# Attention with two MLPs on one core: loads and first conversions of K and V tied to the low part of P

## The chip, the cores and the metric

The kernel runs on one core of a Trainium2 chip. The metric is the device time of one execution in microseconds (us). The core has a matrix engine (TensorE, PE in the profile; its weight loads are PEld), a vector engine (VectorE, DVE), a scalar engine (ScalarE, ACT), GpSimd (POOL), a sync engine (SyncE, SP) that here issues nearly all transfers, and 16 DMA engines that carry them out.

## The reference

Four batches of 8 heads, 576 positions, head size 64. Causal attention is mixed with a memory read-out, and the result (2304 rows of 512) goes through two MLPs of width 2048.

```python
scores = scale * np.matmul(q, k.transpose(0, 1, 3, 2))
...
local = np.matmul(a, v)
...
return (g * mem_out + (1 - g) * local).astype(np.float32)
...
h = x @ w_in
g = np.maximum(h, 0.0) + np.log1p(np.exp(-np.abs(h)))
return (g @ w_out).astype(np.float32)
...
r = np.maximum(h, 0.0)
g = r * r
return (g @ w_out).astype(np.float32)
```

`a` is the softmax of the masked scores, and the MLP weights come as 64-bit floats.

## The kernel before

Every operand is split into a high 16-bit part and a low part (the rest), and a product is made of three matmuls (high by high, high by low, low by high).

The 2304 rows are 18 chunks of 128, numbered from 0: two batches at a time, four full chunks of each in turn, then one chunk of the two remainders (chunks 8 and 17). A chunk attends to its own and the earlier chunks of its batch, so chunks 0 to 8 and 9 to 17 are two halves that share nothing. A chunk is worked on in attention steps: 2 steps for chunks 0, 1, 9 and 10, 4 for 2, 3, 11 and 12, 8 for the others, 104 in all.

A step (`attn_step`) records `emit_s` (scores on PE, L311; mask and row maximum on DVE, L316; exponential on ACT, L320), then the part of the preparation of the next chunk that falls into it, then `emit_p`: the high part of P on ACT (L334), the low part on DVE (L335), and the transpose of both by DMA (L197, tile PT). Four steps later `emit_pv` multiplies by V (L359), and after every fourth head `emit_x` finishes rows of x (xt, xf, xn, L385 to L397).

The preparation of a chunk (`prep_part`) has four parts, at the quarters of the chunk before: K (`prep_k`: high part on ACT, L230, low part on DVE, L231, transpose into KT by DMA), q, phi of q, and V (`prep_v`: ACT L238, DVE L239). After a part has used its raw tile (rawk, rawq, rawv, one buffer of each; a second one for the first K) it asks for the next chunk's load (`load`, L181, on SP). KT and V have 9 buffers each.

The first MLP's weights come in 32 pieces of 512 KB (tile wst, three buffers). A piece is decoded in three DVE instructions (wcv, L428 to L430), its high part W is made on ACT (L432), its low part on DVE (L433). The first MLP's matmuls (L445 to L447 into hps, L462 to L464 into xps, L507 to L509 into xacc) are recorded in units between the attention steps, by a table of costs. For chunks 0 and 1 transposes are made on PE (L203) and copied by ACT (L204), x of these chunks among them; later ones go by DMA. When attention has ended its memory is given to the weights of the second MLP, which are loaded and decoded in the same way; the second MLP follows.

The program is recorded in this order and then ordered anew: a scheduler keeps a list of ready instructions per engine and takes them by priority (`tc.high_priority`), with a model of their times. The order it makes is fixed; on the chip each engine executes its own list in order, and semaphores hold it where its data is not there. `tc.add_manual_dep` with `NoSync` gives the scheduler an edge between two instructions and makes no semaphore. The kernel before has such an edge in `emit_pv`, to the entry of `p_lo` two steps after its own.

Of the kernel before, what the change touches and what calls it, by code (L numbers as in the profile page):

```python
# [13 lines left out]
AF = mybir.ActivationFunctionType  # L14
# [19 lines left out]
TP = 2  # L34

KVB = 9
SPB = 2
WCB = 2
NST = 3
# [11 lines left out]
def kernel(  # L51
# [15 lines left out]
    pe, act, dve, pool, sp = nc.tensor, nc.scalar, nc.vector, nc.gpsimd, nc.sync  # L67
# [58 lines left out]
    for m in (mask[:, 0, 3 * P:], mask[:, 1, EMAX // 2 - P:EMAX // 2]):  # L126
        pool.affine_select(
            out=m, in_=m, pattern=[[-1, P]], compare_op=ALU.is_ge, fill=-8.0e9, base=0, channel_multiplier=1,
# [35 lines left out]
    raw, qT, phiT, KT, V, Mt, Pt, PT, pvt, cs_t = ({} for _ in range(10))  # L164

    def segs(g):
        x = CH[g]
        if len(x) == 2:
            return [(x[0], P * x[1], 0, P)]
        return [(2 * x[0] + i, 4 * P, i * R, R) for i in range(2)]  # L170

    def lo_eng(g):
        return dve if g < LOE else pool

    def load(nm, g, pool_=None):
        if g >= NC or (nm, g) in raw:
            return
        src = {"q": q, "k": k, "v": v}[nm]
        t = (pool_ or att).tile([P, H, D], F32, name="raw" + nm, bufs=1)
        for b, s0, r0, n in segs(g):  # L180
            sp.dma_start(out=t[r0:r0 + n], in_=src[b, :, s0:s0 + n, :].rearrange("h p d -> p h d"))  # L181
        raw[nm, g] = t
    def load_m(g):
        for b, s0, r0, n in (segs(g) if g < NC else []):
# [6 lines left out]
    def transp(g, out, in_, lim):  # L191
        nblk = in_.shape[1] // P
        if g >= lim:
            step = nblk if nblk <= 12 else nblk // 2
            for a in range(0, nblk, step):
                e = a + step
                sp.dma_start_transpose(out=out[:, a:e], in_=in_[:, a * P:e * P])  # L197
            return
        for a in range(0, nblk, 8):
            e = min(nblk, a + 8)  # L200
            ps = mm.tile([P, 8, P], F16, tag="mm", name="tps")
            for i in range(a, e):
                pe.transpose(ps[:, i - a], in_[:, i * P:(i + 1) * P], ident)  # L203
            act.activation(out[:, a:e], ps[:, :e - a], AF.Copy)  # L204
# [22 lines left out]
    def prep_k(g):  # L227
        r = raw.pop(("k", g))
        kn = att.tile([P, H, 2, D], F16, name="kn")
        act.activation(kn[:, :, 0, :], r, AF.Copy)  # L230
        lo_eng(g).tensor_tensor(kn[:, :, 1, :], r, kn[:, :, 0, :], ALU.subtract)  # L231
        KT[g] = att.tile([P, H, P], F16, name="KT", bufs=KVB)
        transp(g, KT[g], kn.rearrange("p h t d -> p (h t d)"), TP)

    def prep_v(g):
        r = raw.pop(("v", g))
        V[g] = att.tile([P, 2, H, D], F16, name="V", bufs=KVB)
        act.activation(V[g][:, 0], r, AF.Copy)  # L238
        dve.tensor_tensor(V[g][:, 1], r, V[g][:, 0], ALU.subtract)  # L239

    def prep_m(g):
# [44 lines left out]
    def emit_s(g, h0):  # L286
# [34 lines left out]
                pf, pf, AF.Exp, bias=cs[:, 0, h:h + 1], scale=-1.0, accum_out=cs[:, 1, h:h + 1],  # L321
            )
        Pt[g, h0] = p

    p_lo = []

    def emit_p(g, h0):
        G, ext = GRP[g], EXT[g]
# [108 lines left out]
    def unit_h(kb, fp):  # L437
        ps = mm.tile([P, 2, NB], F32, tag="mm", name="hps")
        x = x_at(kb)
        for i in range(2):  # L440
            f = 2 * fp + i
            o = ps[:, i]
            for c in range(NCC):
# [3 lines left out]
                pe.matmul(o, wl, x[:, c], start=False, stop=(c == NCC - 1))  # L447
        a = w1p.tile([P, 2, NB], F32, name="spa", bufs=SPB)
        act.activation(a, ps, AF.Abs)
# [68 lines left out]


    load("k", 0)  # L520
    load("q", 0)
    load("k", 1, stage)
    load("v", 0)
    gates()
# [7 lines left out]
    def prep_part(g, part):  # L532
        if g >= NC:
            return
        if part == 0:
            prep_k(g)
            load("k", g + 1)
        elif part == 1:
            prep_q(g)
        elif part == 2:  # L540
            prep_phi(g)
            load("q", g + 1)
        elif part == 3:
            prep_v(g)
            load("v", g + 1)
            prep_m(g)
            load_m(g + 1)

    prep_k(0)
    prep_q(0)  # L550
    prep_phi(0)
    load("q", 1)
    prep_v(0)
    load_m(0)
    load("v", 1)
# [460 lines left out]
```

## Time and profile before

| what | value |
|---|---|
| timed runs | 957.05, 959.77, 960.59 us (median 959.77) |
| span of the profiled execution, first to last instruction | 953.8 us |
| mean granted clock of TensorE | 0.970 |
| PE busy | 869.4 us (91%) |
| PE weight loads busy | 728.7 us (76%) |
| DVE busy | 737.9 us (77%) |
| ACT busy | 612.4 us (64%) |
| queue that SP issues to, share of the 16 DMA engines | 52.1% |

The page gives the profiled execution as its span; the timed runs include what lies around it. Busy shares are means over stages with different limits: the attention and the first MLP run together up to about 540 us, the second MLP's weights are decoded up to about 640 us, and the second MLP fills the rest.

### The profile page before, as it was taken

What the parts mean: (1) busy time and instruction counts of PE and PEld (TensorE: products, weight loads), DVE (VectorE), ACT (ScalarE), POOL (GpSimd) and SP (SyncE); (2) the same over time, 40 slices, a digit from 0 to 9 for tenths busy, and PEclk for the clock granted to TensorE, in tenths of its full rate; (3) what the DMA queues carried; (4) which work ended last, traced back from release to release, by engine and by line L of the source; (5) the groups of instructions that cost most, each with busy time, mean ns of one, the idle gap of its engine ahead of it and who ended that gap; (6) DMA issues with size and microseconds to landing.
All of it is one profiled execution on the core that took longest, in us unless ns stands there. A gap on an engine that the chain in (4) does not pass through costs nothing.

```text
span 953.8 us, 24659 instructions
## 1 busy us (share of the span) xinstructions
PE 869.4 (91%) x10380; PEld 728.7 (76%) x10380; DVE 737.9 (77%) x1490; ACT 612.4 (64%) x1144; POOL 2.2 (0%) x10
## 2 busy tenths in 40 slices
PE   4434999989999889999999998999999999999998
PEld 3233889878878788899988887544695999999993
DVE  7997999878647767575855599999998998867640
ACT  7864888778759677786957466563356656544530
POOL 0000000000000000000000000000000000000000
PEclk9955999999999999999999999999999999999999
DMA  9999997778698986547664575610000000000001
GB/s 235 234 239 221 219 190 150 118 131 134 101 150 162 182 134 109 96 82 116 92 103 79 133 215 162 200 41 23 23 2 12 13 23 2 24 24 2 24 13 34
DMA packets 285024, 101.25 MB, mean 106 GB/s; under 512 B 248048, under 2 KB 284400, under 8 KB 284912
## 3 DMA queue, kind: packets, MB, share of 16 engines
q1 hardware_dynamic: 284672, 99.65, 52.1%
q8 instruction: 81, 1.33, 0.6%
q14 instruction: 31, 0.25, 0.1%
q10 hardware_dynamic: 240, 0.02, 0.0%
HBM read 48.78 MB, written 4.72 MB: 56 GB/s over the span
## 4 chain that ended last, share of the span: by engine, by line
PE 47%; DVE 9%; ACT 6%; DMA 5%; issue 3%; SPq 1%; DVEq 0%; ACTq 0%
PE h2ps L821 4%; PE h2ps L822 4%; PE h2ps L823 4%; PE ops L883 3%; PE ops L882 3%; PE ops L881 3%; PE hps L447 2%; PE hps L446 2%; PE hps L445 2%; PE s_ps L311 2%; PE xps L463 2%; PE xps L464 2%; PE xps L462 2%; PE h2ps L738 1%; PE ops L918 1%
## 5 line engine op out<-in xcount | busy, mean ns | idle before, releaser
L445 PE MATMUL hps<-x,W 128*128 128x256 f16 x576 | 157.1, 275 | 5.8 <-ACT x L204 4.4
L446 PE MATMUL hps<-x,W 128*128 128x256 f16 x576 | 157.8, 275 | 0.5 <-ACT x L488 0.3
L447 PE MATMUL hps<-x,W 128*128 128x256 f16 x576 | 157.8, 275 | 0.0
L463 PE MATMUL xps<-g,W 128*128 128x256 f16 x512 | 138.7, 273 | 2.1 <-DVE g L456 2.1
L462 PE MATMUL xps<-g,W 128*128 128x256 f16 x512 | 137.1, 273 | 3.4 <-ACT g L455 3.4
L464 PE MATMUL xps<-g,W 128*128 128x256 f16 x512 | 138.7, 273 | 0.0
L311 PE MATMUL s_ps<-KT,qT 128*128 128x128 f16 (+2 forms) x992 | 80.1, 224 | 38.6 <-DVE cs L316 38.1
L320 ACT ACTIVATE Pt<-Pt,cs 128x128 f32<-128x128 f32 (+4 forms) x144 | 84.0, 584 | 43.0 <-DVE cs L316 42.8
L311 PEld LDWEIGHTS <-qT 128*128 128x128 f16 (+1 forms) x992 | 58.4, 105 | 50.2 <-issue 43.9
L335 DVE TENSOR_TENSOR p<-Pt,p 128x512 f16<-128x512 f32 (+2 forms) x104 | 69.2, 665 | 33.7 <-ACT p L334 33.6
L316 DVE CUSTOM_DVE_ANT_0 Pt<-s_ps,mask 128x128 f32<-128x128 f32 (+3 forms) x128 | 61.7, 482 | 9.1 <-PE s_ps L311 8.6
L334 ACT ACTIVATE p<-Pt 128x512 f16<-128x512 f32 (+2 forms) x104 | 62.9, 605 | 5.7 <-DMA PT<-p 4.5
L446 PEld LDWEIGHTS <-W 128*128 128x128 f16 x576 | 56.7, 98 | 12.7 <-issue 6.1
L432 ACT ACTIVATE W<-wcv 128x512 f16<-128x512 f32 x64 | 40.0, 625 | 40.3 <-DVE wcv L430 31.0
L447 PEld LDWEIGHTS <-W 128*128 128x128 bf16 x576 | 56.7, 98 | 7.3 <-issue 0.8
L445 PEld LDWEIGHTS <-W 128*128 128x128 f16 x576 | 56.7, 99 | 6.5
L359 PE MATMUL pvt<-V,PT 128*128 128x64 f16 (+1 forms) x1392 | 59.4, 197 | 0.5 <-DMA PT<-p 0.5
L456 DVE TENSOR_TENSOR g<-spa,g 128x512 f16<-128x512 f32 x72 | 49.2, 685 | 12.9 <-ACT g L455 12.7
L452 DVE SCALAR_TENSOR_TENSOR spa<-hps,spa 128x512 f32<-128x512 f32 x72 | 49.3, 686 | 11.6 <-ACT spa L451 11.5
L462 PEld LDWEIGHTS <-W 128*128 128x128 f16 x512 | 49.9, 98 | 9.4 <-issue 4.2
L464 PEld LDWEIGHTS <-W 128*128 128x128 bf16 x512 | 50.1, 98 | 8.1 <-issue 2.7
L359 PEld LDWEIGHTS <-PT 128*128 128x128 f16 (+1 forms) x1392 | 51.6, 104 | 4.2 <-issue 1.5
(230 smaller groups left out, 2551.8 us busy)
## 6 DMA issues: line engine op xcount, KB each, us to landing
wst<-in_moe_w_in_dram SPq DMA_DIRECT2D x32, 512.0 KB, 4.7
wst<-in_moe_w_out_dram SPq DMA_DIRECT2D x32, 512.0 KB, 4.2
rawk<-in_k_dram SPq DMA_DIRECT2D x16, 256.0 KB, 4.3
rawq<-in_q_dram SPq DMA_DIRECT2D x16, 256.0 KB, 4.2
rawv<-in_v_dram SPq DMA_DIRECT2D x16, 256.0 KB, 4.2
out_dram<-T SPq DMA_DIRECT2D x12, 256.0 KB, 2.5
PT<-p SPq DMA_TRANSPOSE x100, 3.4
mraw<-in_M_prev_dram SPq DMA_DIRECT2D x8, 128.0 KB, 4.6
```

The costliest lines, as they stand in the source:

```text
L311: pe.matmul(o[x * n:(x + 1) * n], qT[g][:, t * H + h, x * n:(x + 1) * n], KT[kb][:, h, a - j * P:e - j * P], start=(t == 0), stop=(t == 1),)
L316: dve.tensor_tensor_reduce(out=pw, in0=view, in1=mw, scale=-0.125, scalar=3.0e38, op0=ALU.add, op1=ALU.min, accum_out=cs[:, 0, h:h + 1],)
L320: act.activation(pf, pf, AF.Exp, bias=cs[:, 0, h:h + 1], scale=-1.0, accum_out=cs[:, 1, h:h + 1],)
L334: act.activation(v16[:, :, 0], p, AF.Copy)
L335: p_lo.append(dve.tensor_tensor(v16[:, :, 1], p, v16[:, :, 0], ALU.subtract).ins.name)
L359: m = pe.matmul(o[r], t[:, o0 + i + y, r], V[kb][:, z, h, :], start=(i == 0 and y + z == 0), stop=(i == nb - 1 and y > 0),)
L445: pe.matmul(o, wh, x[:, c], start=(c == 0), stop=False)
L446: pe.matmul(o, wh, x[:, NCC + c], start=False, stop=False)
L447: pe.matmul(o, wl, x[:, c], start=False, stop=(c == NCC - 1))
L462: pe.matmul(ps, wh, gh, start=(f == f0), stop=False)
L463: pe.matmul(ps, wh, gl, start=False, stop=False)
L464: pe.matmul(ps, wl, gh, start=False, stop=(f == f1 - 1))
```

## The change

`hold` gives the scheduler an edge from the load of K and V and from their first conversion, for chunks from 4 on, to the low part of P that was recorded last at that point. `p_lo`, the list of these, moves up so that `load` sees it. No instruction is added or removed and no semaphore is asked for.

```diff
+KVH = 4
...
+    p_lo = []
+
+    def hold(g, m):
+        if g >= KVH and p_lo:
+            tc.add_manual_dep(
+                m.ins, p_lo[-1],
+                mybir.DependencyInfo(mybir.DependencyClass.NoSync, mybir.DependencyReason.DATA),
+                reason="keys and values not before",
+            )
...
-            sp.dma_start(out=t[r0:r0 + n], in_=src[b, :, s0:s0 + n, :].rearrange("h p d -> p h d"))
+            m = sp.dma_start(out=t[r0:r0 + n], in_=src[b, :, s0:s0 + n, :].rearrange("h p d -> p h d"))
+            if nm != "q":
+                hold(g, m)
...
     def prep_k(g):
...
-        act.activation(kn[:, :, 0, :], r, AF.Copy)
+        hold(g, act.activation(kn[:, :, 0, :], r, AF.Copy))
...
     def prep_v(g):
...
-        act.activation(V[g][:, 0], r, AF.Copy)
+        hold(g, act.activation(V[g][:, 0], r, AF.Copy))
...
-    p_lo = []
```

Lines of the changed kernel are numbered 11 to 13 higher than the same lines before. Three places show how the order moves.

ACT, where x of chunk 1 is copied out of PSUM (L204, in the changed kernel L217) for the first matmul of the first MLP. Before:

```order
107 L396 ACTIVATE xn<-xf 128x512
108 L432 ACTIVATE W_70<-wcv 128x4x128
109 L320 ACTIVATE Pt,cs<-Pt,cs 128x256
110 L334 ACTIVATE p_1_102<-Pt 128x2x256
111 L238 ACTIVATE V<-rawv 128x512
112 L204 ACTIVATE x_61<-tps 128x8x128
```

and now:

```order
98 L407 ACTIVATE xn<-xf 128x512
99 L333 ACTIVATE Pt,cs<-Pt,cs 128x256
100 L345 ACTIVATE p_1_102<-Pt 128x2x256
101 L217 ACTIVATE x_61<-tps 128x8x128
102 L333 ACTIVATE Pt,cs<-Pt,cs 128x256
103 L443 ACTIVATE W_70<-wcv 128x4x128
104 L333 ACTIVATE Pt,cs<-Pt,cs 128x256
105 L345 ACTIVATE p_0_101<-Pt 128x2x256
106 L251 ACTIVATE V<-rawv 128x512
```

The conversion of V (of chunk 8 before, of chunk 4 now) stood right ahead of the copy of x and now stands five rows behind it.

SP, around the transposes of P of steps 8 and 9 (PT from p; the weight pieces are wst). Before:

```order
57 L197 DMA_TRANSPOSE PT<-p_0_101 128x8x128
58 L409 DMA wst<-in_moe_w_in_dram 128x4x128
59 L197 DMA_TRANSPOSE KT<-kn 128x8x128
60 L181 DMA rawk<-in_k_dram 128x8x64
61 L197 DMA_TRANSPOSE PT<-p_1_102 128x8x128
62 L409 DMA wst<-in_moe_w_in_dram 128x4x128
63 L181 DMA rawv<-in_v_dram 128x8x64
```

and now:

```order
41 L210 DMA_TRANSPOSE qT<-qn 128x8x128 x2
42 L210 DMA_TRANSPOSE PT<-p_0_101 128x8x128
43 L420 DMA wst<-in_moe_w_in_dram 128x4x128 x3
44 L210 DMA_TRANSPOSE PT<-p_1_102 128x8x128
45 L192 DMA rawv<-in_v_dram 128x8x64
46 L210 DMA_TRANSPOSE PT<-p_0_101 128x8x128
47 L420 DMA wst<-in_moe_w_in_dram 128x4x128
```

Between the two transposes of P a K transpose and a K load are gone, and three weight loads (pieces 17 to 19) stand together behind the first of them.

ACT in the second half, around x of chunk 10 (xn). Before:

```order
445 L238 ACTIVATE V<-rawv 128x512
446 L334 ACTIVATE p_0_101<-Pt 128x2x256
447 L488 ACTIVATE x_62<-xps 128x4x128
448 L396 ACTIVATE xn<-xf 128x512
449 L320 ACTIVATE Pt,cs<-Pt,cs 128x256
450 L238 ACTIVATE V<-rawv 128x512
451 L449 ACTIVATE spa<-hps 128x512
```

and now:

```order
437 L407 ACTIVATE xn<-xf 128x512
438 L333 ACTIVATE Pt,cs<-Pt,cs 128x256
439 L499 ACTIVATE x_62<-xps 128x4x128
440 L345 ACTIVATE p_0_101<-Pt 128x2x256
441 L333 ACTIVATE Pt,cs<-Pt,cs 128x256
442 L251 ACTIVATE V<-rawv 128x512
443 L460 ACTIVATE spa<-hps 128x512
```

Two conversions of V (chunks 14 and 15) stood within six rows; one is left, that of chunk 12.

## Rows read from the trace of the kernel before

**Rows 1.** The page's head and its first line of busy time.

```profile
span 953.8 us, 24659 instructions
...
PE 869.4 (91%) x10380; PEld 728.7 (76%) x10380; DVE 737.9 (77%) x1490; ACT 612.4 (64%) x1144; POOL 2.2 (0%) x10
```

**Rows 2.** Busy us of each engine by stretch, instructions, granted clock, DMA share, GB/s.

```profile
0.00:40.00 40.00, 17.58 (x154) 13.16 (x155) 33.41 (x88) 33.10 (x71) 2.23 (x10) 1.00 1.10 233
40.00:93.00 53.00, 18.51 (x227) 14.81 (x225) 46.66 (x120) 32.39 (x73) 0.00 (x0) 0.53 1.15 231
93.00:174.00 81.00, 79.61 (x954) 71.18 (x954) 78.59 (x179) 66.96 (x140) 0.00 (x0) 0.97 0.89 183
174.00:262.00 88.00, 81.27 (x1200) 71.97 (x1198) 65.56 (x143) 69.63 (x141) 0.00 (x0) 1.00 0.73 121
262.00:375.00 113.00, 102.28 (x1299) 90.04 (x1299) 77.09 (x198) 86.24 (x199) 0.00 (x0) 1.00 0.89 150
375.00:540.00 165.00, 164.48 (x2265) 146.28 (x2263) 105.69 (x231) 119.81 (x241) 0.00 (x0) 1.00 0.55 90
540.00:594.00 54.00, 50.92 (x464) 45.18 (x463) 48.34 (x87) 30.09 (x51) 0.00 (x0) 1.00 0.66 203
594.00:954.00 360.00, 354.73 (x3833) 276.05 (x3831) 282.58 (x451) 174.22 (x233) 0.00 (x0) 1.00 0.10 32
```

**Rows 3.** ACT in order of time: start, us, what, [idle before <- who ended it].

```profile
56.44 0.63 ACT L230 ACTIVATE kn<-rawk 128x512 f16<-128x512 f32 x1 [2.84 <-DMA rawk<-in_k_dram]
...
67.39 0.63 ACT L230 ACTIVATE kn<-rawk 128x512 f16<-128x512 f32 x1 [2.67 <-DMA rawk<-in_k_dram]
...
79.23 0.63 ACT L238 ACTIVATE V<-rawv 128x512 f16<-128x512 f32 x1 [2.74 <-DMA rawv<-in_v_dram]
...
91.31 0.63 ACT L238 ACTIVATE V<-rawv 128x512 f16<-128x512 f32 x1 [4.62 <-DMA rawv<-in_v_dram]
91.84 1.01 ACT L204 ACTIVATE x<-tps 128x1024 f16<-128x1024 f16 x1
```

**Rows 4.** PE in order of time: the first matmul of the first MLP.

```profile
92.90 0.37 PE L445 MATMUL hps<-x,W 128*128 128x256 f16 x1 [4.42 <-ACT x L204]
```

**Rows 5.** DVE in order of time.

```profile
48.49 0.69 DVE L231 TENSOR_TENSOR kn<-rawk,kn 128x512 f16<-128x512 f32 x1
49.09 0.69 DVE L429 SCALAR_TENSOR_TENSOR wcv<-wst,wcv 128x512 int32<-128x512 int32 x1
...
68.05 0.69 DVE L231 TENSOR_TENSOR kn<-rawk,kn 128x512 f16<-128x512 f32 x1 [0.72 <-ACT kn L230]
...
79.89 0.69 DVE L239 TENSOR_TENSOR V<-rawv,V 128x512 f16<-128x512 f32 x1 [1.19 <-ACT V L238]
...
85.47 0.69 DVE L397 TENSOR_TENSOR xn<-xf,xn 128x512 f16<-128x512 f32 x1
...
91.97 0.69 DVE L239 TENSOR_TENSOR V<-rawv,V 128x512 f16<-128x512 f32 x1 [2.92 <-ACT V L238]
...
174.38 0.69 DVE L433 TENSOR_TENSOR W<-wcv,W 128x512 bf16<-128x512 f32 x1
```

**Rows 6.** ACT in order of time, in the second half.

```profile
316.72 0.63 ACT L230 ACTIVATE kn<-rawk 128x512 f16<-128x512 f32 x1 [0.89 <-DMA rawk<-in_k_dram]
...
341.39 0.63 ACT L238 ACTIVATE V<-rawv 128x512 f16<-128x512 f32 x1 [4.35 <-DMA rawv<-in_v_dram]
```

**Rows 7.** The chain that ended last, 310 to 345 us: start, us, what.

```profile
312.98 3.66 DMA rawk<-in_k_dram
...
335.84 5.53 DMA rawv<-in_v_dram
```

**Rows 8.** Waits of DVE: us in total, times, longest us.

```profile
DVE wcv L428 <- DMA wst<-in_moe_w_in_dram: 6.5, 1, 6.5
```

**Rows 9.** The chain that ended last, behind the end of attention.

```profile
540.05 5.17 DMA wst<-in_moe_w_in_dram
```

## The prediction

> **What bounds the kernel now.** I read the page's head first. The profiled execution spans 953.8 us and TensorE (PE) is busy for 869.4 of them [rows 1], so about 84 us of the span are its idle time. The table by stretches then says where that idle time lies [rows 2]. Up to 93 us PE is busy 17.6 of 40 and 18.5 of 53 us, and in that second part it gets 0.53 of its clock. From 93 to 174 it stands for 1.4 us, from 174 to 262 for 6.7, from 262 to 375 for 10.7, from 375 to 540 for 0.5, from 540 to 594 for 3.1. So the first 93 us and the stretch around 300 us are where time can come from, and elsewhere PE is full and whatever comes earlier ahead of it moves the rest of the kernel with it.
>
> What holds PE in the first 93 us is read from the other engines. VectorE (DVE) is busy 46.7 of 53 us between 40 and 93, and the DMA engines are booked at 1.15 of their time [rows 2]. ScalarE (ACT) is busy only 32.4 of those 53 us, and its rows in order of time say why [rows 3]: it executes in order, and it stands in front of conversions of K and V whose raw data has not landed, 2.84 us, 2.67, 2.74 and 4.62. These belong to chunks 6, 7, 7 and 8. The chunk being worked on at that time is 2 or 3, so nobody needs them. Behind the last of them stands the copy of x that the first matmul of the first MLP waits for: that matmul starts at 92.90 after PE stood 4.42 us for the copy [rows 4]. The same pattern comes again in the second half of the batches: ACT stands 4.35 us for V of chunk 15 and 0.89 for K of chunk 16 [rows 6], and there the loads themselves are on the chain that ended last, 3.66 and 5.53 us [rows 7].
>
> **The change part by part.** Nothing is removed and nothing is added: 14 of 18 chunks get their K and V loads and first conversions tied to the low part of P that was recorded last. The tie is one of scheduling alone, so no semaphore is added and no engine gets a new wait; what changes is the order on ACT, DVE, SP and PE. On SP the loads go later and with them the K transposes; GpSimd is not touched. I count in that order with the 18 chunks numbered from 0.
>
> *Up to 174 us.* I take the subtraction that finishes the 32nd (last) weight piece of the first MLP as the mark, because the matmuls of its first block cannot pass their weights; it starts at 174.38 [rows 5]. Ahead of it stand 10 K and 9 V subtractions before, 7 and 7 now: 5 fewer. One takes 0.69 us, but the next starts 0.60 after it (48.49 to 49.09 [rows 5]), so 5 x 0.60 = 3.0 us. DVE also stood for K and V of chunks 7, 7 and 8 behind ACT's waits: 0.72 + 1.19 + 2.92 = 4.8 us [rows 5]. Those conversions now stand after the mark or long after their load. DVE is busy 78.6 of 81 us from 93 to 174 [rows 2], so what leaves its queue moves the mark: -7.8 us. Lower bound -3.0, if other waits take the place of the removed ones. Upper bound is what the start of the dense matmuls gains: 8 K and V subtractions fewer ahead of the second x chunk (9 + 8 before, 5 + 4 now; 4.8 us), the 0.72 + 1.19 us of waits that lie ahead of it at 85.47, and the 4.62 us that ACT stands before the copy: 11.3 us. I take 7.8 because PE, started earlier, then meets the weights.
>
> *174 to 262 us.* Five of the moved conversions land here (K of chunks 7 to 9, V of 7 and 8). One costs ACT about 0.53 us (91.31 to 91.84 [rows 3]) and DVE 0.60. ACT is busy 69.6 of 88 us here and DVE 65.6 [rows 2]. Between 0 (all of it in ACT's idle time) and 5 x (0.53 + 0.60) = 5.7 us (each in series with the chain of an attention step) I take ACT's part times the share of time in which ACT is occupied, 5 x 0.53 x 0.79 = +2.1 us.
>
> *262 to 375 us.* Before, 17 K and V conversions stand here; now 8 of them (K and V of chunks 14 to 17) go past it. Two waits of ACT on the chain go with them, 4.35 and 0.89: -5.2 us. Bounds: 0, if q's loads and transposes are what is late next, and the 10.7 us that PE stands here.
>
> *375 to 540 us.* Those 8 conversions come back here. PE stood for 0.5 us of 165 with ACT at 119.8 and DVE at 105.7 [rows 2]; PE has MLP matmuls to cover with. I take twice its idle time: +0.5 us; bounds 0 and 8 x 1.13 = 9.0 us, if the cover is gone.
>
> *From 540 us.* The second MLP's weights start to load when attention has ended (540.05 [rows 9]); the same rows follow in the same order, so this part only shifts: 0.
>
> The transfers move too. Ahead of the copy of x, three K loads, four V loads and three K transposes leave SP's queue while the DMA engines are booked at 1.15 [rows 2]. I give that no term of its own; it is part of why the removed waits should not come back elsewhere.
>
> Sum: -7.8 + 2.1 - 5.2 + 0.5 = -10.4 us. Against the profiled span that is 953.8 to 943.4. The median of the three timed runs is 959.8, 6.0 above that span; the same difference gives 949.4 us.
>
> A rule speaks against the change. What the trace shows first: V of chunk 8, needed only chunks later, is loaded early, and ACT meets it at 91.31 before it has landed [rows 3], while the DMA engines are booked beyond their time [rows 2]. The Trainium skill, "DMA: Bandwidth & Descriptors", section "Rules for kernel authors", says to issue a DMA early and wait on it late, so that its fixed cost overlaps. By it the sum would be worse than mine, and the fourth rival below prices that; the rows of before disagree with it where the early wait sits in an in-order queue.
>
> **The rivals.**
> 1. *More than forecast.* PE keeps the whole 11.3 us of its earlier start, the idle time around 300 us goes entirely and nothing comes back: -22.0, 937.8 us. For it: PE was full from 93 to 174. Against: the last weight pieces move by less than that.
> 2. *Eaten by half-time.* The K subtraction of chunk 10 has about as many DVE instructions ahead of it before and now (536 and 540). If the chain of attention and not PE sets when that point comes, the early gain is returned by 270 us and only the second half pays: -5.2 + 0.5, 955.1 us. Against: DVE and ACT are at 0.75 and 0.79 between 174 and 262 and PE at 0.92 [rows 2].
> 3. *Slower: weight pieces come late.* On SP four weight loads (pieces 17, 20, 24 and 26) now stand behind transposes of P that wait for DVE, and between the point that lets them go and DVE's first use lie only 17, 18, 13 and 15 DVE instructions, some 8 to 11 us. A weight load took 5.17 us on the chain [rows 9], so they should fit. If they don't, DVE, which works in order, stands for the piece; the one such wait in the trace is 6.5 us [rows 8]. Four of them: +26, 975.4 us. It decides from about 4 us a piece, where gain and loss are equal within 0.5%.
> 4. *The late loads are waited for.* Counted from the last transpose of P ahead of a load on SP, the order leaves 43 and more DVE instructions before nearly every held load's conversion, where it was 12 to 37 for nearly all of the second half before. The exceptions are V of chunks 10 and 11 and K of 11 (22 to 34). Two waits as in [rows 6] would give 949.4 + 2 x 4.35 = 958.1 us. This is what the Trainium skill's rule on early issue would do here.
>
> That the tie does nothing is excluded: the order has changed.
>
> **How the numbers follow.** A measurement of this kernel can tell about 0.5% (4.8 us) from no change. Chances: forecast 0.58, rival 1 0.15, rival 2 0.13, rival 3 0.09, rival 4 0.05. Faster by over 0.5%: forecast and rival 1, 0.73. Within 0.5%: rivals 2 and 4, 0.18. Slower: rival 3, 0.09. The range goes from rival 1 to rival 4, 938 to 958 us; it leaves out rival 3 and some of the far sides of rivals 1 and 2. The bounds of the terms alone would reach from -22.0 to +11.7.
>
> **What would show it.** Right: the first MLP matmul starts at about 81 to 84 us and not at 92.9; no ACT wait on rawk or rawv over 1 us between 45 and 93 or after 320; the last weight subtraction of the first MLP at about 167; PE idle of 174 to 262 up by 2 us at most; fewer than 6 us of PE idle around 300; attention ends near 528. Wrong: the matmuls start earlier but the last weight piece does not (then DVE waits for something else), or DVE rows of the weight conversion that wait for their loads, or PE idle time after 375 us in place of the idle time before.

## The result and the profile after

Six runs of each gave 950.12 us (946.51 to 953.34) against 957.96 us for the kernel before (956.81 to 960.59): ratio 0.9907, 95% interval 0.9881 to 0.9933. In a later comparison (a_again below) nine runs of the changed kernel gave 949.36 us against 954.94, 0.9933 (0.9908 to 0.9958). So the change gains 0.7 to 0.9%, 6 to 9 us; 10.4 were forecast. The profiled execution took 953.34 us, the slowest of its six, with a span 1.8 us below that. The span of the profile before is 953.8 us [rows 1], so these two traces lie only 2.3 us apart and show less of the gain than the runs do; for the main readings the profile of a_again (span 945.8 us), "the second profile", is set beside the first.

The head of the page and its first line of busy time, to be read beside [rows 1]:

```profile
span 951.5 us, 24644 instructions
...
PE 873.7 (92%) x10371; PEld 730.7 (77%) x10380; DVE 737.6 (78%) x1490; ACT 613.6 (64%) x1144; POOL 2.2 (0%) x10
```

The busy totals are those of before within 0.5% (PE 4.3 us more): the same work in another order. The table by stretches, with the columns of [rows 2]:

```profile
40.00:93.00 53.00, 32.02 (x368) 25.59 (x366) 49.54 (x134) 37.42 (x84) 0.00 (x0) 1.00 0.97 213
93.00:174.00 81.00, 74.52 (x914) 67.54 (x912) 76.42 (x172) 64.85 (x135) 0.00 (x0) 1.00 0.98 180
174.00:262.00 88.00, 79.50 (x1179) 69.18 (x1179) 68.21 (x144) 70.41 (x142) 0.00 (x0) 0.98 0.83 145
262.00:375.00 113.00, 107.06 (x1316) 94.73 (x1316) 74.56 (x195) 84.26 (x192) 0.00 (x0) 0.97 0.78 131
375.00:540.00 165.00, 160.58 (x2206) 142.34 (x2204) 105.01 (x228) 119.01 (x240) 0.00 (x0) 1.00 0.64 101
540.00:594.00 54.00, 51.57 (x455) 45.07 (x454) 50.72 (x91) 31.75 (x54) 0.00 (x0) 0.97 0.68 208
```

The 1.00 in the clock column of the first line cannot be right: the first matmuls of the first MLP start 0.21 us apart up to 83 us, as they do before at a granted clock of 0.50 up to 98 us, and 0.11 us apart behind that. In the second profile the column reads 0.59 there, against 0.53 before.

PE works 13.5 us more between 40 and 93 and 4.8 more between 262 and 375, and less in the three other stretches up to 540: 5.1 us from 93 to 174, 1.8 from 174 to 262, 3.9 from 375 to 540. The first gain is what [rows 3, 4] promised. PE in order of time, the first matmul of the first MLP (92.90 before):

```profile
79.19 0.37 PE L456 MATMUL hps<-x,W 128*128 128x256 f16 x1 [0.69 <-ACT x L217]
```

Waits of ACT for K and V between 40 and 93 us (us in total, times, longest), before:

```profile
ACT V L238 <- DMA rawv<-in_v_dram: 7.8, 3, 4.6
ACT kn L230 <- DMA rawk<-in_k_dram: 6.0, 3, 2.8
```

and after, where this is all that is left of them:

```profile
ACT V L251 <- DMA rawv<-in_v_dram: 1.4, 1, 1.4
```

The end of the stage answers to the last of [rows 5], the 32nd weight subtraction on DVE:

```profile
169.50 0.68 DVE L444 TENSOR_TENSOR W<-wcv,W 128x512 bf16<-128x512 f32 x1
```

The mark came 4.9 us earlier (174.38 before), not 7.8; in the second profile 5.8. Single traces scatter here: f2_from14, with the order of before up to 300 us, has the mark at 173.4. The table by stretches from the start to the mark, before and after, with DVE's busy time in the third place behind the length:

```profile
0.00:174.38 174.38, 116.08 (x1335) 99.49 (x1336) 159.03 (x385) 132.82 (x283) 2.23 (x10) 0.84 1.01 209
```

```profile
0.00:169.50 169.50, 119.69 (x1368) 102.25 (x1369) 155.96 (x381) 131.61 (x279) 2.23 (x10) 1.00 1.01 203
```

DVE is busy 3.1 us less ahead of the mark, which is the 3.0 of the forecast for the subtractions, but it stands only 1.8 us less (2.5 in the second profile), where 4.8 were forecast. Two new waits of DVE make the difference. The first is for the 17th weight piece, whose load SP issues, first of three, right behind a transpose of P; DVE, and then SP:

```profile
82.50 0.43 DVE L439 TENSOR_SCALAR wcv<-wst 128x512 int32<-128x512 int32 x1 [2.92 <-DMA wst<-in_moe_w_in_dram]
```

```profile
76.53 1.82 SPq L210 DMA_TRANSPOSE PT<-p  x1
78.40 1.67 SPq L420 DMA_DIRECT2D wst<-in_moe_w_in_dram  x3
```

The profile before has no wait of DVE for a weight piece up to 110 us. The second wait is for a high part of P; ACT, which makes it, and DVE, which makes the low part from it:

```profile
115.16 0.52 ACT L345 ACTIVATE p<-Pt 128x384 f16<-128x384 f32 x1 [3.60 <-DMA PT<-p]
```

```profile
115.72 0.56 DVE L346 TENSOR_TENSOR p<-Pt,p 128x384 f16<-128x384 f32 x1 [2.71 <-ACT p L345]
```

ACT makes the high part late because it stands 3.60 us for a transpose: P has two buffers, and the high part of a step is written over the one that the transposes of two steps before must have read. This wait grows in the rest of attention too. Waits of ACT for transfers of q, K, V and P between 93 and 540 us, before:

```profile
ACT qn L221 <- DMA rawq<-in_q_dram: 12.0, 7, 3.5
...
ACT V L238 <- DMA rawv<-in_v_dram: 7.8, 3, 4.3
...
ACT p L334 <- DMA PT<-p: 4.5, 7, 1.3
...
ACT kn L230 <- DMA rawk<-in_k_dram: 3.8, 3, 1.8
```

and after, where rawk and rawv have no row at all:

```profile
ACT p L345 <- DMA PT<-p: 16.6, 12, 3.6
ACT qn L234 <- DMA rawq<-in_q_dram: 15.8, 9, 3.4
...
ACT phie L268 <- DMA rawq<-in_q_dram: 1.6, 1, 1.6
```

So what ACT no longer waits for K and V (11.6 us) it waits for P's buffer instead (12.1 us more), and for q it waits 5.4 us more. Whether the wait for P's buffer matters is what the third buffer below tests.

### The profile page after: what moved, and what is told of

It is laid out like the page before. It is cut to its first block, busy times and chain, and to the rows that moved or that the text cites. A ratio compares the mean times of both kernels' runs of the same rounds, so it can differ in the third digit from the quotient of the medians.

```text
span 951.5 us, 24644 instructions
## 1 busy us (share of the span) xinstructions
PE 873.7 (92%) x10371; PEld 730.7 (77%) x10380; DVE 737.6 (78%) x1490; ACT 613.6 (64%) x1144; POOL 2.2 (0%) x10
## 4 chain that ended last, share of the span: by engine, by line
PE 62%; DVE 13%; DMA 12%; ACT 8%; issue 4%; SPq 0%; ACTq 0%; DVEq 0%
DMA PT<-p 4%; PE h2ps L832 4%; PE h2ps L833 4%; PE h2ps L834 4%; DMA rawq<-in_q_dram 4%; PE hps L457 4%; PE hps L458 3%; PE hps L456 3%; PE ops L892 3%; PE ops L894 3%; PE ops L893 3%; PE xps L473 3%; PE xps L474 3%; PE xps L475 3%; PE s_ps L324 3%
## 5 line engine op out<-in xcount | busy, mean ns | idle before, releaser
L474 PE MATMUL xps<-g,W 128*128 128x256 f16 x512 | 140.1, 275 | 1.8 <-DVE g L467 1.8
L473 PE MATMUL xps<-g,W 128*128 128x256 f16 x512 | 139.4, 276 | 1.3 <-ACT g L466 1.2
L475 PE MATMUL xps<-g,W 128*128 128x256 f16 x512 | 140.1, 275 | 0.0
L345 ACT ACTIVATE p<-Pt 128x512 f16<-128x512 f32 (+2 forms) x104 | 63.1, 607 | 18.0 <-DMA PT<-p 16.6
L467 DVE TENSOR_TENSOR g<-spa,g 128x512 f16<-128x512 f32 x72 | 49.3, 685 | 13.5 <-ACT g L466 13.4
```

Of the source, the lines that this page charges most:

```text
L345: act.activation(v16[:, :, 0], p, AF.Copy)
L473: pe.matmul(ps, wh, gh, start=(f == f0), stop=False)
L474: pe.matmul(ps, wh, gl, start=False, stop=False)
L475: pe.matmul(ps, wl, gh, start=False, stop=(f == f1 - 1))
```

## The experiments

Each was timed in five rounds against the kernel before on the same chip; there are three chips, four kernels on each. The edits are against the changed kernel if not said otherwise. "PE idle" is the length of a stretch less PE's busy time in it, by the table by stretches of each run's profile:

| | tied | ratio (95%) | 93–174 | 174–262 | 262–375 | 375–540 | ACT for P's buffer, 93–540 |
|---|---|---|---|---|---|---|---|
| before | none | 1 | 1.4 | 6.7 | 10.7 | 0.5 | 4.5 |
| the change, first profile | 4 to 17 | 0.9907 (0.9881–0.9933) | 6.5 | 8.5 | 5.9 | 4.4 | 16.6 |
| a_again | 4 to 17 | 0.9933 (0.9908–0.9958) | 5.1 | 7.2 | 6.2 | 4.0 | 14.6 |
| e1_first | 4 to 8 | 0.9954 (0.9936–0.9972) | 4.8 | 7.3 | 7.2 | 0.6 | 14.1 |
| k1_mid | 9 to 13 | 1.0019 (1.0003–1.0036) | 1.3 | 5.9 | 3.6 | 3.1 | 10.6 |
| f2_from14 | 14 to 17 | 0.9953 (0.9936–0.9970) | 1.5 | 6.7 | 6.0 | 1.8 | 6.2 |
| e2_second | 9 to 17 | 1.0000 (0.9979–1.0021) | 0.3 | 6.8 | 2.8 | 2.3 | 7.5 |
| f1_to14 | 4 to 13 | 0.9972 (0.9957–0.9986) | 6.1 | 6.2 | 8.7 | 1.5 | 15.4 |
| f3_both | 4 to 8, 14 to 17 | 0.9936 (0.9913–0.9959) | 5.1 | 5.9 | 6.2 | 4.5 | 14.1 |
| e4_load | 4 to 17, loads only | 0.9928 (0.9909–0.9947) | 5.6 | 5.1 | 7.0 | 1.8 | 6.3 |
| e6_v8 | V of 8, conversion only | 1.0053 (1.0030–1.0076) | 5.8 | 5.7 | 9.3 | 1.1 | 7.2 |
| h1_before_p3 | none, third buffer | 0.9969 (0.9955–0.9984) | 2.3 | 5.7 | 8.0 | 0.2 | 0 |
| g1_p3 | 4 to 17, third buffer | 0.9875 (0.9849–0.9901) | 5.7 | 4.6 | 4.7 | 1.4 | 0 |
| h3_both_p3 | 4 to 8, 14 to 17, third buffer | 0.9870 (0.9850–0.9891) | 3.9 | 5.5 | 5.7 | 1.1 | 0 |

Idle times are of one execution each, and the stretches are fixed in time while the work moves under them; a difference under 1 us says nothing.

**The change again.** No edit.

> The change itself once more beside the other three on one chip, for a common base: 0.990 to 0.993 of the kernel before. In the trace the stretch from 375 to 540 us again has some 4 us of PE idle time, if the moved conversions cause it; 1 us or less if it was chance.

It repeats: 0.9933, and the 4.0 us of PE idle time in 375 to 540 are there again. That stretch is where the forecast was off most.

**The halves apart.**

```diff
-        if g >= KVH and p_lo:
+        if KVH <= g < 9 and p_lo:
```

> Only chunks 4 to 8 are tied (first half); the order up to the last chunk of the first half is that of the change. Theory A (two gains that stand apart): -7.8 + 2.1 = about -5.7 us against the kernel before, 0.994. Theory B (the early gain is eaten by half-time): within 1.5 us of before, and the 52nd low part of P no earlier than in the kernel before. Theory C (all comes from the first half, the second changes nothing): the full -7.8 us.

```diff
-KVH = 4
+KVH = 9
```

> Only chunks 9 to 17 are tied (second half); the order up to about 110 us is that of the kernel before. Theory A: -5.2 + 0.5 = about -4.7 us, 0.995; the trace then has under 6 us of PE idle time between 262 and 375 us. Theory B: the whole -7.8 us. Theory C: within 1.5 us of before.

The first half alone gives 0.9954, 4.4 us of 955, with an interval from 2.7 to 6.1 us: theory A, whose 5.7 lies in it. The second half alone gives nothing, although its trace has only 2.8 us of PE idle time around 300, as theory A wanted; in time it is theory C for that half. So is the whole second half worthless? The next three take it apart.

**The second half in parts.** In f1_to14 and f2_from14:

```diff
-        if g >= KVH and p_lo:
+        if KVH <= g < 14 and p_lo:
```

> Chunks 4 to 13 are tied, chunks 14 to 17 are not. The order is that of the change up to the preparation of chunk 14; from there K and V of chunks 14 to 17 are converted early again (17 and 14 of them ahead of step 64, against 14 and 14 with the change and 18 and 18 before). Theory G (the tied conversions of chunks 14 to 17 are what gave time back in 375 to 540): PE idle from 375 to 540 at most 1 us (the change 4.0 to 4.4, before 0.5), idle from 262 to 375 back at 7 to 11 us, end of attention 6 to 7 us earlier than before, and in time what the first half alone gave, 0.995. Rival M (what was given back comes from meeting chunk 9 to 13's work later): idle of 3 to 4 us in 375 to 540 stays. Rival S (the halves' gains add and nothing is given back): 0.991 or better for the change itself, this one between it and 0.995.

```diff
-KVH = 4
+KVH = 14
```

> Only chunks 14 to 17 are tied: the order is that of before for the first 589 instructions of DVE, and then K and V of chunks 14 to 17 stand where the change has them (14 and 14 ahead of step 64). This is my term for 262 to 375 and that for 375 to 540 without the rest. By the prediction's sizes: -5.2 +0.5 = -4.7 us, 0.995. Theory G (given back): PE idle from 262 to 375 falls from 10.7 to 3 to 6 us, rises from 0.5 to 2.5 to 4 us in 375 to 540, the chain that ended last goes through the conversions of V and K on ACT between 440 and 490 us, and the time is 0.998 to 1.001. Rival: idle in 375 to 540 stays under 1 us and the whole -4.7 us is kept.

and in k1_mid:

```diff
-        if g >= KVH and p_lo:
+        if 9 <= g < 14 and p_lo:
```

> Only chunks 9 to 13 are tied. The runs so far give their part as quotients: 1.0047 (9 to 17 over 14 to 17) and 1.0018 (4 to 13 over 4 to 8). Theory P: slower than before, 1.001 to 1.005, with PE idle of 174 to 375 not smaller than the 17.4 us of before, or more ACT waits on P's buffer. Rival (the quotients are scatter between chips): 0.998 to 1.000.

Chunks 14 to 17 alone gain 4.5 us by the ratio and 5.0 by the medians (956.39 to 951.39), which is the forecast of -5.2 + 0.5 for the two stretches that they concern; theory G, which wanted 0.998 to 1.001, fell, and so did a detail of its rival, since the idle time from 375 to 540 is 1.8 us and not under 1. For f1_to14 theory G was right about the idle time around 300 (8.7 us) and not about the time, 0.9972. Chunks 9 to 13 alone cost 0.2%, and the interval just leaves out no change. Adding them to 14 to 17 moves 0.9953 to 1.0000, which is clear of the intervals; adding them to 4 to 8 moves 0.9954 to 0.9972, which is not (in either pair the two ran on different chips). So tying these five chunks buys nothing in these runs, and costs something alone and beside 14 to 17. The three parts sum to -0.46 + 0.19 - 0.47 = -0.74%, within the intervals of the whole.

What makes 9 to 13 dear is not shown. k1_mid has ACT standing 10.6 us for P's buffer where it was 4.5, but e2_second only 7.5. And idle time is not the whole account: the span of e2_second's profile holds 76.5 us of PE idle time where the one before holds 84.4, but 874.8 us of PE busy time where that holds 869.4, for the same matmuls. The last section has one thing that lengthens PE's busy time.

**Without the dear part.**

```diff
-        if g >= KVH and p_lo:
+        if (KVH <= g < 9 or g >= 14) and p_lo:
```

> Chunks 4 to 8 and 14 to 17 are tied, chunks 9 to 13 are not. Alone the first gave 0.9954 and the last 0.9953. Theory P (they act in different halves and add, and what the change loses is lost by tying 9 to 13): 0.9907, PE idle of 262 to 375 at 3 to 6 us. Rival G (ties of 14 to 17 cost more when the first half comes early, because PE then has no work of the MLP to cover with): 0.993 to 0.9955, and PE idle of 3 to 4 us in 375 to 540.

The time is 0.9936, rival G's, where the product of the two good parts is 0.9907; with intervals of 0.0017 to 0.0023 on each of the three, the times alone do not rule out that the parts add. The idle time speaks for rival G: PE stands 4.5 us in 375 to 540 where each alone has 0.6 and 1.8. Taking out 9 to 13 is no better than the change.

**The third buffer for P.** In the changed kernel, in the one without ties, and with the ties of f3_both:

```diff
-P16 = 2
+P16 = 3
...
-    p16 = [att.tile([P, 2 * EMAX], F16, name=f"p16_{i}") for i in range(P16)]
+    p16 = [att.tile([P, 2 * EMAX if i < 2 else 1024], F16, name=f"p16_{i}") for i in range(P16)]
...
-        t16 = p16[pcount[0] % len(p16)]
+        t16 = p16[pcount[0] % (3 if G * w <= 512 else 2)]
```

> The change with a third buffer of 1024 columns for the two parts of P, used by the steps that need no more than that (all but those of chunks 8 and 17). The early term fell short of its size (32nd weight subtraction 4.9 to 6.2 us earlier, not 7.8): in the traces of the change DVE stands 1.7 to 2.7 us near 115 us for the high part of P, which ACT makes late because it waits 3.6 us for the transposes by DMA to have read the buffer; ACT stands 4 to 5 us for such transposes between 90 and 174. Theory T (that wait took the place of the removed ones): with three buffers the wait is gone, the 32nd weight subtraction comes 7 to 9 us earlier than before, and the time falls by another 1 to 3 us, ratio 0.989 to 0.992. Rival (PE or the weights are the limit there, or the transposes are late for those who read them as well): the wait on P's buffer goes, another takes its place, and the ratio is that of the change, 0.993.

> The kernel before with the third buffer for the parts of P, and no tie. In the trace of before ACT stands 4.5 us between 93 and 540 for the transposes of P that have to read the buffer, in the change 14.6 us (first half tied alone 14.1). Theory T (the tie moves the load off and lets ACT come to P's buffer before it is free, so that this wait ate part of the gain): without the tie there is little to win, 0.996 to 1.000, and the gain of the two together (0.9875) is more than the product of each alone (0.993 times this). Rival (the third buffer is worth the same with and without the tie): 0.9942, the quotient of 0.9875 and 0.9933.

> The same ties (4 to 8 and 14 to 17) with the third buffer for the parts of P. If the ties of 9 to 13 cost time with three buffers as well: 0.983 to 0.986, better than 0.9875. If what they cost was only the wait on P's buffer: 0.986 to 0.989, the same as with all of them.

The wait on P's buffer is gone in all three. The order of ACT's instructions is the same with and without the third buffer all through attention, and DVE's but for a few places, so what these runs compare is the buffer. Without ties it is worth 0.3%. With them it is 0.9870 against 0.9936 on the chip that also ran h1_before_p3, and 0.9875 against the 0.9933 of a_again: 0.6 to 0.7%. Against the first measurement of the change, 0.9907, it is 0.3%.

That the buffer is worth more with the tie, the times do not show. If the two effects merely multiplied, 0.9969 would make 0.9905 of 0.9936, 0.9902 of 0.9933 and 0.9876 of 0.9907; the runs gave 0.9870 (up to 0.9891) and 0.9875 (up to 0.9901). It rests on the traces. PE idle time from 93 to 540 falls by 3.1 us without the tie (19.4 to 16.3), by 6.1 with it (22.5 to 16.4) and by 5.6 in f3_both (21.7 to 16.1), and the 4.0 and 4.5 us of 375 to 540 become 1.4 and 1.1. Counted from the 60th low part of P to the 72nd, so that it does not matter where the work stands in time, PE idles 3.6 us in both profiles of the change and 3.2 in f3_both, and 0.3 and 0.0 with the third buffer (g1_p3, h3_both_p3); without ties it is 2.8 with two buffers and 1.8 with three. The table by stretches of a_again:

```profile
262.00:375.00 113.00, 106.75 (x1294) 95.26 (x1292) 73.83 (x194) 84.18 (x193) 0.00 (x0) 0.98 0.83 133
375.00:540.00 165.00, 161.02 (x2208) 142.70 (x2207) 106.81 (x230) 119.42 (x241) 0.00 (x0) 1.00 0.64 107
```

and of the change with the third buffer:

```profile
262.00:375.00 113.00, 108.26 (x1356) 97.33 (x1355) 76.60 (x202) 87.05 (x200) 0.00 (x0) 1.00 0.81 133
375.00:540.00 165.00, 163.63 (x2204) 145.42 (x2203) 110.83 (x233) 116.87 (x232) 0.00 (x0) 1.00 0.67 118
```

The chain that ended last shows one place where it is lost, in a_again (start, us, what):

```profile
355.99 0.60 DVE p L346
...
357.00 5.50 DMA PT<-p
362.59 0.53 ACT p L345
363.14 0.56 DVE p L346
...
370.13 4.56 DMA rawq<-in_q_dram
```

The transposes of one P take 5.50 us, ACT stands 2.96 us for their buffer, the next low part of P is late by that, and the load of q, which follows on SP, lands 2.86 us after ACT came to it. The same conversion of q in the kernel with three buffers, ACT in order of time:

```profile
366.81 0.63 ACT L234 ACTIVATE qn<-rawq 128x512 f16<-128x512 f32 x1 [1.08 <-DMA rawq<-in_q_dram]
```

No wait for P stands ahead of it and 1.08 us are left for q. From the 60th low part of P to the 72nd this kernel takes 52.9 us, a_again 56.7.

The early expectation of g1_p3 fell, though: its 32nd weight subtraction is 6.2 us earlier than before, not 7 to 9, hardly better than the 5.8 of a_again. The wait for P is gone, but the one for the 17th weight piece is still there, 2.9 us here and 2.9 to 3.5 us in all seven profiles in which chunks 4 to 8 are tied as in the change. Whether it alone keeps the mark from coming 7 to 9 us earlier, no run tried. The third buffer pays later, between 174 and 400 us. And no cost of the ties of 9 to 13 is seen once it is there (0.9875 with them, 0.9870 without, on two chips).

**Loads alone.**

```diff
-        hold(g, act.activation(kn[:, :, 0, :], r, AF.Copy))
+        act.activation(kn[:, :, 0, :], r, AF.Copy)
...
-        hold(g, act.activation(V[g][:, 0], r, AF.Copy))
+        act.activation(V[g][:, 0], r, AF.Copy)
```

> Only the loads of K and V are tied; their first conversions are free, so they come about one chunk earlier than in the change (6 and 5 of K and V ahead of the second x chunk instead of 5 and 4; 15 and 15 instead of 14 and 14 ahead of step 64). Theory A (what counts is that ACT does not meet a conversion whose load has just been issued): a conversion that is free to follow its late load at once is met before the data has landed, so ACT waits of 2 to 5 us on rawk or rawv come back between 45 and 93 us, and about half of the gain of the change is lost: 0.996 to 0.999. Rival L (what counts is that the loads leave SP's queue and the DMA engines early on): the gain of the change stays, 0.992 to 0.994, and the first matmul of the first MLP starts at 79 to 82 us.

This one corrects the reason, not the number. Theory A's waits did come back. ACT, 93 to 540 us:

```profile
ACT kn L243 <- DMA rawk<-in_k_dram: 13.2, 9, 3.2
...
ACT V L251 <- DMA rawv<-in_v_dram: 3.9, 3, 1.5
```

With 6.0 us in 40 to 93 that is 23.1 us of standing for K and V, nearly the 25.4 of before (13.8 + 11.6), and still the time is that of the change, 0.9928: rival L. With the waits for P's buffer ACT stands 29.4 us here, 29.9 in the kernel before and 15.6 in a_again (with those for q, 42.0, 44.1 and 32.3), so the length of ACT's waits does not set the time. What this kernel shares with the change is the early start: its first MLP matmul is at 81.5 us, with three K and three V conversions fewer ahead of the second x chunk. Rival L's reason, the loads that leave SP's queue, is not shown apart from this, since the conversions come later with their loads. That a wait costs only what stands behind it and is waited for is my reading; no run tried it by itself.

**One conversion alone.** Only the conversion of V of chunk 8, the one with the 4.62 us wait of [rows 3], is tied; the other two calls of `hold` are taken out:

```diff
-        if g >= KVH and p_lo:
+        if g == 8 and p_lo:
```

> Only the conversion of V of chunk 8 is tied, the one that stands ahead of the copy of x; every other conversion stays early. If the in-order wait of ACT is what counts at the start: first matmul of the first MLP some 4 us earlier (at about 88 us) and the last weight piece 2.9 us earlier, so about -3 us in all. If the DVE instructions that leave the queue are what counts: the first matmul about 4 us earlier, the last weight piece within 1 us of before and the total within 1 us.

It is slower, 1.0053. Its first MLP matmul starts at 88.7 us, 4.2 earlier, but the 32nd weight subtraction at the same time as before, as the second expectation had it: between 93 and 180 ACT now stands 3.4 us for K of chunk 9, where it stood 1.8, and DVE 1.9 behind it; and DVE stands 1.5 us for the 18th weight piece. The wait moved on. Neither expectation had the time right, and why it ends 4 to 5 us above the kernel before, and not level with it, stays open.

## Why the prediction was right, and where not

*What bounds the kernel.* Right. PE's idle time went where [rows 2] said it could come from, ahead of 93 us and around 300. That "no engine gets a new wait" holds for semaphores only: the new order brought a wait for a weight piece that was not there, and longer ones for P's buffer and for q.

*Up to 174 us, -7.8.* The mechanism was right, the size not: -4.9, and -5.8 in the second profile. The term for the subtractions came out as forecast, 3.1 us of busy time less for 3.0. The step that failed is the other one, that the 4.8 us of removed waits would not come back: DVE stands only 1.8 and 2.5 us less ahead of the mark, because it waits 2.9 us (3.2 in the second profile) for the 17th weight piece and 2.7 (1.7) for P's high part. The lower bound allowed for that ("if other waits take the place of the removed ones"); the value taken did not. The start of the matmuls moved by 13.7 us, more than the 11.3 of the upper bound, and most of it was lost again by 174.

*174 to 262 us, +2.1.* PE idle time +1.8 and +0.5: right in sign and, in the first profile, in size. The two terms of the first half, -5.7 together, were -4.4 us timed (e1_first).

*262 to 375 us, -5.2.* PE idle time -4.8 and -4.5: right, and f2_from14 confirms it in time together with the next term. Less idle time here is not yet time, though: e2_second has 7.9 us less and gains nothing.

*375 to 540 us, +0.5.* Mis-sized inside its bounds of 0 and 9.0: +3.9 and +3.5 measured. "PE has MLP matmuls to cover with" holds when chunks 14 to 17 alone are tied (+1.3), and no longer when the first half is tied too. The runs put P's buffer in its place: with a third one, and the same conversions in the stretch (seven, not eight, with two buffers and with three), the idle time is 1.4 and 1.1.

*From 540 us, 0.* Nothing speaks against it: DVE's 64th weight subtraction is as much earlier than before as the end of attention is, within 1.5 us (1.4 and 2.9 in the first profile, 6.8 and 6.8 in the second).

*The sum.* -10.4 against -6 to -9. The forecast in us came out 0.7 from the median partly by luck: the three runs of before that it was hung on had a median of 959.8, and with three more it was 958.0. As a ratio the forecast was 0.9892, inside the first interval and outside the second. By the traces (the shift of the mark and the changes of PE's idle time) the four terms are -4.0 us together in the first profile and -6.3 in the second: the two that missed their size most, the first and the fourth, were both too hopeful.

*The signs.* The first MLP matmul came at 79.2 and 78.3 us, earlier than the 81 to 84 named; one wait on rawv of 1.4 and 1.0 us was left ahead of 93, and none was left after 320; the mark came at 169.5 and 168.6, not at 167; the idle time from 174 to 262 rose by less than the 2 us named, and that around 300 was 5.9 and 6.2, at the 6 named. The first load of the second MLP's weights, which [rows 9] have at 540.05, started at 537.1 and 533.2, so attention did not end near 528. Two of the signs of being wrong were there in part: a row of the weight conversion that waits for its load, and PE idle time after 375 us.

*The rivals.* Rival 1 (more) did not come. Rival 2 (eaten by half-time) fell: the 52nd low part of P, at 273.7 us before, is 7.3 and 9.3 us earlier, and the first half alone gains. Rival 3 (late weight pieces) came for one of its four pieces, the 17th, with 2.9 and 3.2 us, less than the 4 us a piece at which it would have decided; it took part of the first term and not the gain. Rival 4 (late loads waited for) fell: there is no ACT wait on rawk or rawv after 93 us. The rule of the Trainium skill that stood behind it ("DMA: Bandwidth & Descriptors", "Rules for kernel authors") asks for early issue and a late wait; here the early issue was not needed, and e4_load shows it most plainly, since tying the issue alone gives 0.9928. A rival that I did not have came as well: a wait for another buffer, P's, in place of the waits for K and V.

## What to carry to other kernels

On an engine that executes in order, don't price waits by their sum: a kernel with 29 us of waits for K, V and P's buffer and one with 16 took the same time here (0.9928 and 0.9933). Ask of each what stands behind it and who waits for that. When a reordering lets an engine come earlier, look at once at the next buffer that it will meet, count its copies and its reader's time, and try one more of it together with the reordering: here the two gave 0.9875 where the reordering alone gave 0.9933 and 0.9907. Look as well at the loads that now stand behind others in a queue, such as the 17th weight piece here. And time the parts of a tie apart before trusting the whole, since one of three parts here, alone, gained nothing and cost 0.2%.

## What the runs showed of the hardware

TensorE's granted clock fell to half (1.2 of 2.4 GHz) for 3.4 us in the middle of full work, right behind idle times of 1.3 to 2.4 us. The table by stretches of the changed kernel around one of them:

```profile
192.00:195.80 3.80, 0.82 (x10) 0.61 (x10) 2.95 (x7) 2.83 (x7) 0.00 (x0) 1.00 0.97 183
195.80:199.20 3.40, 3.33 (x16) 2.31 (x16) 2.90 (x8) 3.40 (x8) 0.00 (x0) 0.50 0.88 169
199.20:202.60 3.40, 3.40 (x58) 3.15 (x56) 1.91 (x5) 1.24 (x4) 0.00 (x0) 0.99 1.08 208
```

PE did 0.82 us of work in 3.8, with idle times of 1.29 and 1.60 us, and then ran at 0.50 for 3.4 us, 16 matmuls where the next stretch of the same length has 58 (of other shapes in part). The first profile of the change has four such dips (195.8, 274.3, 325.5 and 585.0 us), the profile of before none between 98 us and its last microseconds, e1_first four between 190 and 335 and f2_from14 none. At half the clock each costs 1.7 us of work at most, an estimate from its length, so four of them are of the size of the scatter between executions. The profile before, with none, is not typical: over the runs with a mean granted clock above 0.98 the clock averages 0.9958 for the kernel before (45 runs), 0.9934 for the change (10), 0.9946 for e2_second (10) and 0.9977 for f2_from14 (6); the records of such runs leave out the low clock of the start, which the other runs, at 0.949 to 0.976, count in whole or in part. As an estimate from these means, that is 4.1, 6.3, 5.2 and 2.2 us lost to half clock. So some 2 us of what the tie could gain, and part of what the ties of 9 to 13 cost, may be lost there; no run tried it. Not every idle time of that length is followed by one: in the same profile 1.6 us at 230.5 and 1.9 us at 379.9 are not.
